# Key decay on ScalarE, weight conversion on GpSimd in eight rounds, and hidden slices moved inside the attention loop

## The chip, the cores and the metric

One Trainium2 chip, one of its cores. The metric is device time in microseconds for one execution of the whole kernel, the median of several executions. TensorE (PE) does matmuls, VectorE (DVE) and ScalarE (ACT) work on SBUF and PSUM, GpSimd (POOL) on SBUF, and SyncE (SP) issues the DMAs. Each engine runs its own list of instructions in order and waits for the others by semaphores. Float32 data goes through the matmuls as two rounded parts, a high part and a rest, each in TensorE's `float32r` type.

## The reference

```
q, k, v: (2 batches, 8 heads, 768 tokens, 64); lam: one decay per head
attention, in blocks of tokens:
    out  = (q k^T * lam^(i-j), lower triangle) v  +  (q * lam^(i+1)) state
    state = lam^block * state + (k * lam^(block-1-j))^T v
x (1536 x 512) = out, heads side by side
x  = G(x @ w_in (512 x 2048)) @ w_out          G: 0, (h+1)^2/4, h, piecewise
out = (sigmoid(x @ w_gate) * (x @ w_val)) @ w_out2      d_ff 1536
```

The five weight matrices come as float64 words and are turned into float32 parts on the chip.

## The kernel before

**Attention.** The work is cut into 16 units: two batches, four pairs of heads, two halves of the 768 tokens, each half three blocks of 128 tokens. For unit i: `pre_k` multiplies the keys by the decay column of the table `DT` (tile kd), `pre_q` the queries by `qp` (tile qs); `scores` makes q k^T on PE; `updates` makes the three state updates from kd; `weigh_states` multiplies the scores by `DT` into pT (two DVE instructions, one for each head) and runs the recurrence sc of the states on DVE, then copies them to st on ACT; `outputs` makes the unit's output x on PE from pT, qs and st; `evacuate` splits x into xh (ACT, line 492) and xl (DVE, line 493), the input of the feed-forward. The tables come from a small constant `cs`: `DT` and `qp` of the first two heads are built on chip, the others go through DRAM (`pd`) and come back by DMA.

**The order** is written out by hand: step i of the loop issues scores, updates and states of unit i+1, the decayed keys of unit i+2, then outputs and evacuation of unit i, then the decayed queries of unit i+2. Each engine keeps that order.

**Weight conversion.** The weights are 68 pieces of 128 x 512 words. `w_round` is a pipeline of one piece per stage: round k makes the words of piece k (two ACT copies), the float of piece k-1 (DVE lines 95 and 96, then an integer add, line 98, on DVE or POOL), and the two parts of piece k-2: the high part on ACT (line 102) and the rest (line 106, `w_low`) on DVE or POOL. In the attention loop `ROUNDS` says at which steps a round is issued; afterwards rounds go between the feed-forward's units.

**Feed-forward.** `feed_forward` is a generator of slices: a slice is one 128-wide strip of the hidden layer for 512 tokens, 12 matmuls (`hidden`, lines 150 to 152: high part, rest, high part with xl, for four strips of the input), then an activation (lines 176 to 178), a split of it (gh, gl: lines 168, 169), and `project`, 12 matmuls (line 205). `HIDDEN` says at which steps of the attention loop one slice is made ahead of time; there are four. The 24 matmuls of the first two projects come right after attention, and from there on PE runs the feed-forward.

Of the kernel before, what the change touches and what calls it, by code (L numbers as in the profile page):

```python
# [10 lines left out]
AF = mybir.ActivationFunctionType  # L11
ALU = mybir.AluOpType
PSUM = bass.MemoryType.PSUM

B, H, S, D = 2, 8, 768, 64
NT, DM = B * S, H * D
FF1, FF2 = 2048, 1536
P = 128
NP = H // 2
CU = 3  # L20
# [5 lines left out]
GF = 4  # L26
PADW = 64
CST = 4 + PADW + P
HIDDEN = (7, 9, 11, 13)
ROUNDS = (3, 4, 5, 6, 8, 9, 10, 11, 12, 13, 14)  # L30
NQD = 2
NEARLY = 4
WARM = 2
# [4 lines left out]
def fused_kernel(ctx: ExitStack, tc: tile.TileContext, qkv, qd, cst, w1, w2, out):  # L38
    nc = tc.nc
    pe, act, dve, pool, sp = nc.tensor, nc.scalar, nc.vector, nc.gpsimd, nc.sync  # L40
# [20 lines left out]

    pieces = [(n, o) for n in range(NF1 + NF2) for o in range(0, 1024 if n < NF1 else 1536, 512)]
    pieces[:8] = sorted(pieces[:8], key=lambda no: 2 * no[0] + (3 if no[1] else 0))
    index = {no: i for i, no in enumerate(pieces)}
    raws, ws, tmps = {}, {}, {}

# [3 lines left out]
    def w_load():  # L73
        i = prog["loaded"]
        if i >= len(pieces) or i >= NRAW + max(0, prog["round"] - 2):
            return
        prog["loaded"] += 1
        n, o = pieces[i]
        raws[i] = rawp.tile([P, 512], I64, tag="raw", name=f"raw{i}")
        src = w1[n] if n < NF1 else w2[n - NF1]  # L80
        sp.dma_start(out=raws[i], in_=src[:, o:o + 512])
# [190 lines left out]
    steps = feed_forward(rounds)  # L272


    with ExitStack() as actx:
# [6 lines left out]
        nu = len(units)  # L282
        raw_u = {}

        def u_load(i):
            if i >= nu:
                return
            b, p, h = units[i]
            if i < NEARLY:

                t = [wp.tile([P, 2, 512], F32, tag="w", name=f"u{i}_{j}")
                     .rearrange("p a b -> p (a b)")[:, 0:2 * UT]
                     .rearrange("p (a t) -> p a t", a=2) for j in range(2)]
                for j in range(2):
                    sp.dma_start(out=t[j], in_=qkv[b, p, h][:, 2 * j:2 * j + 2])
            else:
                a = up.tile([P, 4, UT], F32, tag="u", name=f"u{i}")
                sp.dma_start(out=a, in_=qkv[b, p, h])
                t = [a[:, 0:2], a[:, 2:4]]
            raw_u[i] = [t[j // 2][:, j % 2] for j in range(4)]  # L300
# [4 lines left out]
        DT = kp.tile([P, H, P], F32, name="DT")  # L305
# [15 lines left out]
        def tables():  # L321

            cs = tp.tile([P, 512], F32, tag="r", bufs=3, name="cs")
            dm = [tp.tile([P, 512], F32, tag="r", bufs=3, name=f"dm{j}")[:, 0:2 * (PADW + P)]
                  .rearrange("p (h x) -> p h x", h=2) for j in range(2)]
            act.dma_start(out=cs[:, 0:CST], in_=cst)
            for i in range(3):
                u_load(i)
            dve.memset(zero, 0.0)
            for j in range(2):  # L330
                dve.memset(dm[j][:, :, 0:PADW], 0.0)
            dve.memset(half, 0.5)
            pool.memset(pw[:, 0:P - 1], 0.0)
            pool.memset(pw[:, P - 1:P], 1.0)
            pool.memset(st[0], 0.0)
            act.activation(st[1], st[0], AF.Copy)

            act.activation(pw[:, P:P + 1], cs[0:H, 2:3], AF.Copy)
            for k in range(7):
                w = 1 << k  # L340
                act.activation(pw[:, P + w:P + 2 * w], pw[:, P:P + w], AF.Copy,
                               scale=pw[:, P + w - 1:P + w])
            act.dma_start(out=pd, in_=pw)
            act.activation(qp[:, 0, 0:1], cs[:, 3:4], AF.Copy)
            for k in range(7):
                w = 1 << k
                act.activation(qp[:, 0, w:2 * w], qp[:, 0, 0:w], AF.Copy,
                               scale=qp[:, 0, w - 1:w])
            sq = [cs[:, 0:2]] + [cs[:, CST + 2 * k:CST + 2 * k + 2] for k in range(6)]
            for k in range(1, 7):  # L350
                pool.tensor_tensor(out=sq[k], in0=sq[k - 1], in1=sq[k - 1], op=ALU.mult)
            for h in range(2):
                for k in range(7):
                    w = 1 << k
                    src = cs[:, 4:CST] if k == 0 else dm[k % 2][:, h]
                    dve.scalar_tensor_tensor(
                        out=DT[:, h] if k == 6 else dm[(k + 1) % 2][:, h, PADW:],
                        in0=src[:, PADW - w:PADW + P - w], scalar=sq[k][:, h:h + 1],
                        in1=src[:, PADW:], op0=ALU.mult, op1=ALU.add,
                    )  # L360
            pdv = pd[:, :]
            for e in range(2):
                sp.dma_start(
                    out=qp[e * D:(e + 1) * D, 1:],
                    in_=bass.AP(pdv.tensor, pdv.offset + (2 + e) * 2 * P + P,
                                [[0, D], [4 * P, NP - 1], [1, P]]),
                )
            for h0, h1 in ((2, 4), (4, H)):
                sp.dma_start(
                    out=DT[:, h0:h1],  # L370
                    in_=bass.AP(pdv.tensor, pdv.offset + h0 * 2 * P,
                                [[1, P], [2 * P, h1 - h0], [1, P]]),
                )
            u_load(3)
            u_load(4)
            w_load()
            u_load(5)
            w_load()

        S_ps, U_ps, pT, qs, kd, xs = {}, {}, {}, {}, {}, {}  # L380

        def pre_k(i):

            b, p, h = units[i]
            kd[i] = sp2.tile([P, CU, 2, D], F32, tag="kd", name=f"kd{i}")
            pool.tensor_tensor(
                out=kd[i], in0=raw_u[i][2].rearrange("p (c h d) -> p c h d", c=CU, h=2),
                in1=DT[:, 2 * p:2 * p + 2, P - 1:P].unsqueeze(1).to_broadcast([P, CU, 2, D]),
                op=ALU.mult,
            )  # L390

        def pre_q(i):

# [38 lines left out]
        def weigh_states(i):  # L432
            b, p, h = units[i]
            pT[i] = sp2.tile([P, 2, UT], F32, tag="pT", name=f"pT{i}")
            S, t = S_ps.pop(i), U_ps.pop(i)
            sb, sd = sc[p % 2], st[p % 2]
            n0, n1 = h * CU, min(h * CU + CU, 2 * CU - 1)

            def weigh(e):
                dve.tensor_tensor(  # L440
                    out=pT[i][:, e].rearrange("p (c t) -> p c t", c=CU),
                    in0=S[e][:, 0:UT].rearrange("p (c t) -> p c t", c=CU),
                    in1=DT[:, 2 * p + e].unsqueeze(1).to_broadcast([P, CU, P]), op=ALU.mult,
                )

            def state(n):
                u = t[:, (n - n0) * D:(n - n0 + 1) * D]
                if n == 0:
                    dve.tensor_copy(out=sb[:, n], in_=u)
                elif n < n1:  # L450
                    dve.scalar_tensor_tensor(  # L451
                        out=sb[:, n], in0=sb[:, n - 1], scalar=qp[:, p, P - 1:P], in1=u,
                        op0=ALU.mult, op1=ALU.add,
                    )

            weigh(0)
            state(n0)
            weigh(1)
            state(n0 + 1)
            state(n0 + 2)  # L460
            for e in range(2):
                r = slice(e * D, (e + 1) * D)
                act.activation(sd[r, n0:n1, r], sb[r, n0:n1], AF.Copy)  # L463
# [33 lines left out]

        with tc.manual_schedule():
            tables()
            warm()  # L500
            scores(0)
            scores(1)
            pre_k(0)
            pre_k(1)
            updates(0)
            weigh_states(0)
            pre_q(0)
            pre_q(1)


            for i in range(nu):
                if i + 1 < nu:
                    if i:
                        scores(i + 1)
                    updates(i + 1)
                    weigh_states(i + 1)
                if i + 2 < nu:
                    pre_k(i + 2)

                def finish():  # L520
                    outputs(i)
                    evacuate(i)

                if i in ROUNDS:
                    w_round(pool, finish, pool if i >= nu // 2 else dve)
                else:
                    finish()
                if i + 2 < nu:
                    pre_q(i + 2)
                u_load(i + 6)  # L530
                w_load()
                if i in HIDDEN:
                    next(steps)


    late = ctx.enter_context(tc.tile_pool(name="late", bufs=1, reuse_waits="tile"))
# [67 lines left out]
```

## Time and profile before

| | |
|---|---|
| median of 3 runs | 630.03 us (629.92 to 630.14) |
| profiled execution | 630.28 us, of which the span from first to last instruction is 628.3 |
| PE busy | 608.9 us, 97% of the span |
| DVE busy | 356.5 us, 57% |
| ACT busy | 287.8 us, 46% |
| POOL busy | 57.0 us, 9%, all in the first six of the page's 40 slices (94 us) |
| granted PE clock, mean | 0.991 of full speed |

A line of the trace gives the start, the duration, the engine, the source line, the operation and the tiles as out<-in. In brackets stands how long the engine sat idle before it and what ended that. Matmuls are pipelined: the duration of one is longer than the time to the next.

### The profile page before, as it was taken

To read this page: it belongs to the slowest core of one execution; us is meant where nothing else is said; L and a number is where in the kernel's file an instruction comes from. 1 tells how busy PE (TensorE), PEld (TensorE's weight loads), DVE (VectorE), ACT (ScalarE), POOL (GpSimd) and SP (SyncE) were. 2 spreads that over 40 slices of the span, in tenths; PEclk is the share of its full clock that TensorE was granted. 3 is DMA by queue.
4 is the path that set the end of the run, shared out by engine and by line. 5 is a ranking of instruction groups with operands and counts; after the bars stand their busy time and mean duration, and the time that the engine had idled before them with its cause. 6 is when DMAs were issued, how large, how long until landed. Compare 5 with 4: busy or idle time off the path is not lost.

```text
span 628.3 us, 7878 instructions
## 1 busy us (share of the span) xinstructions
PE 608.9 (97%) x3076; PEld 500.8 (80%) x3076; DVE 356.5 (57%) x613; ACT 287.8 (46%) x511; POOL 57.0 (9%) x62
## 2 busy tenths in 40 slices
PE   6978799999999999999999999999999999999997
PEld 4866588888888888888888888888888888888886
DVE  5678876465656665667577721256842167813132
ACT  5457766566546554656484511245631145311110
POOL 4568920000000000000000000000000000000000
PEclk8989999999999999999999999999999999999999
DMA  6967531021203111222222400024420022001011
GB/s 211 413 226 259 211 120 61 23 100 68 68 33 101 66 57 45 70 65 68 67 68 67 135 1 0 1 75 127 134 68 0 1 67 68 1 0 68 0 68 67
DMA packets 15813, 52.59 MB, mean 84 GB/s; under 512 B 1688, under 2 KB 2976, under 8 KB 15776
## 3 DMA queue, kind: packets, MB, share of 16 engines
q1 hardware_dynamic: 15616, 51.98, 24.9%
q8 instruction: 24, 0.39, 0.2%
q10 hardware_dynamic: 160, 0.11, 0.1%
q14 instruction: 13, 0.11, 0.0%
HBM read 48.92 MB, written 3.15 MB: 83 GB/s over the span
## 4 chain that ended last, share of the span: by engine, by line
PE 88%; DVE 6%; ACT 3%; issue 2%; DMA 1%; POOL 0%; ACTq 0%; POOLq 0%
PE a L205 36%; PE h L150 17%; PE h L152 17%; PE h L151 17%; DVE pT L440 2%; DVE sc L451 1%; ACT st L463 1%; ACT xh L492 1%; DMA cs<-in_cst 1%; DVE wr L96 0%; PE x L473 0%; DVE w L106 0%; DVE part L219 0%; DVE xl L493 0%; ACT w L102 0%
## 5 line engine op out<-in xcount | busy, mean ns | idle before, releaser
L150 PE MATMUL h<-xh,w 128*128 128x512 f32 x480 | 187.2, 390 | 1.7 <-ACT xh L492 1.7
L152 PE MATMUL h<-xl,w 128*128 128x512 f32 x480 | 186.9, 389 | 0.0
L151 PE MATMUL h<-xh,w 128*128 128x512 f32 x480 | 186.7, 389 | 0.0
L205 PE MATMUL a<-gh,w 128*128 128x512 f32 x384 | 118.5, 390 | 0.0
L150 PEld LDWEIGHTS h<-xh,w 128*128 128x128 f32 x480 | 90.1, 188 | 20.7 <-ACT xh L492 2.1
L152 PEld LDWEIGHTS h<-xl,w 128*128 128x128 f32 x480 | 90.1, 188 | 19.0 <-DVE xl L493 0.3
L151 PEld LDWEIGHTS h<-xh,w 128*128 128x128 f32 x480 | 90.1, 188 | 18.5
L184 DVE TENSOR_TENSOR r<-r,h 128x512 f32<-128x512 f32 x36 | 24.8, 688 | 138.8 <-PE h L152 138.8
L205 PE MATMUL a<-w,gh 128*128 128x512 f32 x288 | 88.6, 389 | 0.0
L205 PEld LDWEIGHTS a<-gh,w 128*128 128x128 f32 x384 | 71.9, 188 | 15.1 <-issue 0.2
L168 ACT ACTIVATE gh<-r 128x512 fp32r<-128x512 f32 x84 | 52.5, 625 | 63.3 <-DVE r L184 55.7
L178 DVE SCALAR_TENSOR_TENSOR r<-r,h 128x512 f32<-128x512 f32 x48 | 33.0, 687 | 84.6 <-ACT r L177 84.5
L205 PE MATMUL a<-gl,w 128*128 128x512 f32 x192 | 74.7, 389 | 0.0
L176 ACT ACTIVATE r<-h,half 128x512 f32<-128x512 f32 x48 | 33.0, 688 | 90.3 <-PE h L152 90.3
L169 DVE TENSOR_TENSOR gl<-r,gh 128x512 fp32r<-128x512 f32 x84 | 59.1, 704 | 16.6 <-ACT gh L168 16.6
L205 PEld LDWEIGHTS a<-w,gh 128*128 128x128 f32 x288 | 54.0, 188 | 11.2
L183 ACT ACTIVATE r<-h 128x512 f32<-128x512 f32 x36 | 21.5, 597 | 87.0 <-PE h L152 87.0
L102 ACT ACTIVATE w<-wr 128x512 fp32r<-128x512 f32 x68 | 42.3, 623 | 39.7 <-DVE wr L98 39.5
L205 PE MATMUL a<-w,gl 128*128 128x512 f32 x144 | 56.0, 389 | 0.0
L96 DVE SCALAR_TENSOR_TENSOR wr<-raw,wr 128x512 uint32<-128x512 uint32 x68 | 51.2, 753 | 2.3
L88 ACT ACTIVATE wr<-raw 128x512 f32<-128x512 f32 x68 | 45.1, 663 | 0.2 <-POOL w L106 0.2
L89 ACT ACTIVATE wc<-raw 128x512 int32<-128x512 uint32 x68 | 44.9, 660 | 0.0
(52 smaller groups left out, 507.2 us busy)
## 6 DMA issues: line engine op xcount, KB each, us to landing
raw<-in_w SPq DMA_DIRECT2D x68, 512.0 KB, 3.6
u<-in_qkv SPq DMA_DIRECT2D x12, 768.0 KB, 4.7
u<-in_qkv SPq DMA_DIRECT2D x8, 384.0 KB, 5.1
out<-part SPq DMA_DIRECT2D x12, 256.0 KB, 2.1
DT<-pd SPq DMA_DIRECT2D x1, 256.0 KB, 4.2
qp<-pd SPq DMA_DIRECT2D x2, 96.0 KB, 2.8
DT<-pd SPq DMA_DIRECT2D x1, 128.0 KB, 3.8
cs<-in_cst ACTq DMA_DIRECT2D x1, 98.0 KB, 4.1
```

The costliest lines, as they stand in the source:

```text
L88: act.activation(r, hi.bitcast(F32), AF.Copy, scale=2.0 ** -112)
L89: act.activation(c, lo, AF.Copy, scale=2.0 ** -29)
L96: dve.scalar_tensor_tensor(out=ru, in0=hi, scalar=0x80000000, in1=ru, op0=ALU.bitwise_and, op1=ALU.bitwise_or)
L102: act.activation(ws[i][:, 0], tmps[i][1], AF.Copy)
L150: pe.matmul(h, lhsT=wh, rhs=xh[:, k, tt], start=(k == 0), stop=False)
L151: pe.matmul(h, lhsT=wl, rhs=xh[:, k, tt], start=False, stop=False)
L152: pe.matmul(h, lhsT=wh, rhs=xl[:, k, tt], start=False, stop=(k == NP - 1))
L168: act.activation(gh, g, AF.Copy)
L169: dve.tensor_tensor(out=gl, in0=g, in1=gh.bitcast(F32), op=ALU.subtract)
L176: act.activation(r, h, AF.Relu, bias=half, scale=0.5)
L178: dve.scalar_tensor_tensor(out=r, in0=r, scalar=1.0, in1=h, op0=ALU.min, op1=ALU.max)
L205: pe.matmul(accs[j], lhsT=a, rhs=b_, start=(f == 0 and m == 0), stop=(f == GF - 1 and m == 2))
```

## The change

The constant `cs` is loaded first on SP's queue instead of on ACT's, and the fourth unit's inputs come before the tables' DMAs. The decayed keys of units 2 to 15 are two ACT instructions (one for each head) instead of one on POOL; those of units 0 and 1 stay on POOL, in two instructions. Eight rounds instead of eleven are issued in attention, all with integer add and rest on POOL, and the first eight pieces are ordered so that the four pieces for the hidden layer come first and those for the projects after. A slice is issued inside step i, between updates and states of unit i+1 and the outputs of unit i, at steps 8, 10, 12 and 14, and no longer at the end of steps 7, 9, 11 and 13. For the first unit, both weighings come before the states.

```diff
-HIDDEN = (7, 9, 11, 13)
-ROUNDS = (3, 4, 5, 6, 8, 9, 10, 11, 12, 13, 14)
+HIDDEN = (8, 10, 12, 14)
+ROUNDS = (3, 5, 7, 9, 11, 13, 14, 15)
...
-    pieces[:8] = sorted(pieces[:8], key=lambda no: 2 * no[0] + (3 if no[1] else 0))
+    pieces[:2 * GF] = sorted(pieces[:2 * GF], key=lambda no: (no[1], no[0]))
...
-            act.dma_start(out=cs[:, 0:CST], in_=cst)
-            for i in range(3):
+            sp.dma_start(out=cs[:, 0:CST], in_=cst)
+            for i in range(4):
                 u_load(i)
...
-            u_load(3)
             u_load(4)
-            w_load()
             u_load(5)
             w_load()
...
-            pool.tensor_tensor(
-                out=kd[i], in0=raw_u[i][2].rearrange("p (c h d) -> p c h d", c=CU, h=2),
-                in1=DT[:, 2 * p:2 * p + 2, P - 1:P].unsqueeze(1).to_broadcast([P, CU, 2, D]),
-                op=ALU.mult,
-            )
+            for e in range(2):
+                if i < 2:
+                    pool.tensor_tensor(
+                        out=kd[i][:, :, e],
+                        in0=raw_u[i][2].rearrange("p (c h d) -> p c h d", c=CU, h=2)[:, :, e],
+                        in1=DT[:, 2 * p + e, P - 1:P].unsqueeze(1).to_broadcast([P, CU, D]),
+                        op=ALU.mult,
+                    )
+                    continue
+                act.activation(
+                    kd[i][:, :, e],
+                    raw_u[i][2].rearrange("p (c h d) -> p c h d", c=CU, h=2)[:, :, e],
+                    AF.Copy, scale=DT[:, 2 * p + e, P - 1:P],
+                )
...
             weigh(0)
-            state(n0)
-            weigh(1)
+            if i:
+                state(n0)
+                weigh(1)
+            else:
+                weigh(1)
+                state(n0)
...
                     updates(i + 1)
-                    weigh_states(i + 1)
                 if i + 2 < nu:
                     pre_k(i + 2)
+                if i + 1 < nu:
+                    weigh_states(i + 1)
+                if i in HIDDEN:
+                    next(steps)
...
                 if i in ROUNDS:
-                    w_round(pool, finish, pool if i >= nu // 2 else dve)
+                    w_round(pool, finish, pool)
...
                 u_load(i + 6)
                 w_load()
-                if i in HIDDEN:
-                    next(steps)
```

POOL before, in the second third of the attention loop (wr and wc are a weight piece under conversion, w a finished piece; qs and kd are the decayed queries and keys):

```order
L98 TENSOR_TENSOR wr2_465<-wr2_465,wc2_466 128x512
L396 TENSOR_TENSOR qs8_519<-u8_330,qp_92 128x384
L386 TENSOR_TENSOR kd9_548<-u9_377,DT_91 128x384
L396 TENSOR_TENSOR qs9_562<-u9_377,qp_92 128x384
L386 TENSOR_TENSOR kd10_603<-u10_421,DT_91 128x384
L98 TENSOR_TENSOR wr3_514<-wr3_514,wc3_515 128x512
```

POOL of the change, at steps 9 to 13:

```order
L97 TENSOR_TENSOR wr2_553<-wr2_553,wc2_554 128x512
L105 TENSOR_TENSOR w1_660<-wr1_464,w1_660 128x512
L403 TENSOR_TENSOR qs11_667<-u11_470,qp_92 128x384
L403 TENSOR_TENSOR qs12_728<-u12_508,qp_92 128x384
L97 TENSOR_TENSOR wr3_662<-wr3_662,wc3_663 128x512
L105 TENSOR_TENSOR w2_771<-wr2_553,w2_771 128x512
```

The keys are gone from POOL, and a round puts two instructions there, the add of one piece and behind it the rest of the piece before.

PE before, around the first slice (x is a unit's output, h a slice, s the scores, uu the updates):

```order
L425 MATMUL uu_533<-u_330,kd_496 64x64 x6
L473 MATMUL x_550<-pT_489,u_291 64x128 x6
L482 MATMUL x_550<-qs_470,st_99 128x128 x3
L150 MATMUL h_0_0_566<-xh,w_463 128x512
L151 MATMUL h_0_0_566<-xh,w_463 128x512
L152 MATMUL h_0_0_566<-xl,w_463 128x512
```

PE of the change, around the first slice:

```order
L432 MATMUL uu_572<-u_381,kd_525 64x64 x4
L149 MATMUL h_0_0_587<-xh,w_551 128x512
L150 MATMUL h_0_0_587<-xh,w_551 128x512
L151 MATMUL h_0_0_587<-xl,w_551 128x512
...
L151 MATMUL h_0_0_587<-xl,w_551 128x512
L484 MATMUL x_604<-pT_528,u_333 64x128 x6
L493 MATMUL x_604<-qs_506,st_98 128x128 x2
```

The slice now stands ahead of a unit's outputs; before it stood behind them. Its second matmul (line 150 of the change) reads the rest of the weight piece.

DVE before, at the end of attention (pT and sc belong to the last unit, xl to the last two, wr_914 and wr_980 are pieces under conversion):

```order
L440 TENSOR_TENSOR pT_957<-s_1_945,DT 128x384
L451 SCALAR_TENSOR_TENSOR sc_97<-sc_97,qp,uu_952 128x64
L95 TENSOR_SCALAR wr_914<-wr_914 128x512
L96 SCALAR_TENSOR_TENSOR wr_914<-raw_751,wr_914 128x512
L493 TENSOR_TENSOR xl<-x_967,xh 128x384
L95 TENSOR_SCALAR wr_980<-wr_980 128x512
```

DVE of the change at the same place (gl and r are of slices, wr_882 and wr_948 are pieces):

```order
L458 SCALAR_TENSOR_TENSOR sc_97<-sc_97,qp,uu_899 128x64
L168 TENSOR_TENSOR gl_0_925<-r_0_822,gh_0_924 128x512
L177 SCALAR_TENSOR_TENSOR r_0_928<-r_0_928,h_0_0_911 128x512
L94 TENSOR_SCALAR wr_882<-wr_882 128x512
L95 SCALAR_TENSOR_TENSOR wr_882<-raw_562,wr_882 128x512
L504 TENSOR_TENSOR xl<-x_935,xh 128x384
L94 TENSOR_SCALAR wr_948<-wr_948 128x512
L95 SCALAR_TENSOR_TENSOR wr_948<-raw_671,wr_948 128x512
L504 TENSOR_TENSOR xl<-x_958,xh 128x384
```

The float steps of two pieces now stand behind the activation r of the last slice. The end of POOL's list in the change:

```order
L403 TENSOR_TENSOR qs_887<-u_669,qp 128x384
L97 TENSOR_TENSOR wr_882<-wr_882,wc_883 128x512
L105 TENSOR_TENSOR w_946<-wr_773,w_946 128x512
L97 TENSOR_TENSOR wr_948<-wr_948,wc_949 128x512
L105 TENSOR_TENSOR w_970<-wr_882,w_970 128x512
```

Here `w_946` and `w_970` are the pieces that the first two projects read; before, those projects read pieces of the rounds at steps 8 and 10.

## Rows read from the trace of the kernel before

**Rows 1.** Chain of waits, in order of time: start us, us, what.

```profile
0.74 4.11 DMA cs<-in_cst
...
19.69 0.50 ACT xh L492
...
26.28 0.50 ACT xh L492
...
42.65 0.50 ACT xh L492
...
72.89 0.49 ACT xh L492
...
81.17 4.81 PE a L205 x21
```

**Rows 2.** Busy time in two stretches: us, then each engine's, PEclk, DMA.

```profile
0.00:80.53 80.53, 64.87 (x675) 50.62 (x676) 61.27 (x134) 48.35 (x105) 54.56 (x61) 0.94 0.70 257
80.53:622.00 541.47, 541.47 (x2393) 448.42 (x2392) 292.54 (x476) 239.43 (x407) 2.45 (x2) 1.00 0.18 57
```

**Rows 3.** DMA issues of the page, by line, KB, us to landing.

```profile
out<-part SPq DMA_DIRECT2D x12, 256.0 KB, 2.1
```

**Rows 4.** Timeline of the start: start us, us, engine, line, what.

```profile
15.19 0.84 POOL L386 TENSOR_TENSOR kd<-u,DT 128x384 f32<-128x384 f32 x1 [0.98 <-DMA DT<-pd]
```

**Rows 5.** Groups of instructions on ACT by shape: busy us, mean ns.

```profile
L463 ACT ACTIVATE st<-sc 64x192 f32<-64x192 f32 x16 | 5.8, 362 | 12.7 <-DVE sc L451 12.5
...
L341 ACT ACTIVATE pw<-pw 8x64 f32<-8x64 f32 x1 | 0.3, 348 | 0.0
```

**Rows 6.** Timeline of 59 to 69 us, steps 10 to 12.

```profile
59.72 1.29 POOL L98 TENSOR_TENSOR wr<-wr,wc 128x512 int32<-128x512 int32 x1 [1.18 <-DVE wr L96]
...
60.75 0.40 PE L151 MATMUL h<-xh,w 128*128 128x512 f32 x1
...
60.96 1.29 POOL L106 TENSOR_TENSOR w<-wr,w 128x512 fp32r<-128x512 f32 x1
...
61.49 1.04 DVE L95 TENSOR_SCALAR wr<-wr 128x512 uint32<-128x512 uint32 x1
...
62.37 0.49 ACT L492 ACTIVATE xh<-x 128x384 fp32r<-128x384 f32 x1
...
62.89 0.63 ACT L102 ACTIVATE w<-wr 128x512 fp32r<-128x512 f32 x1
...
63.02 0.39 PE L152 MATMUL h<-xl,w 128*128 128x512 f32 x1
...
64.56 0.62 ACT L168 ACTIVATE gh<-r 128x512 fp32r<-128x512 f32 x1
...
68.48 0.63 ACT L463 ACTIVATE st<-sc 64x128 f32<-64x128 f32 x2 [2.07 <-DVE sc L451]
```

**Rows 7.** Timeline of 28 to 46 us, steps 3 to 8.

```profile
28.59 0.42 DVE L95 TENSOR_SCALAR wr<-wr 128x512 uint32<-128x512 uint32 x1
...
29.04 0.69 DVE L96 SCALAR_TENSOR_TENSOR wr<-raw,wr 128x512 uint32<-128x512 uint32 x1
...
29.88 1.28 POOL L98 TENSOR_TENSOR wr<-wr,wc 128x512 int32<-128x512 int32 x1 [1.43 <-PE x L473]
...
44.33 0.69 ACT L176 ACTIVATE r<-h,half 128x512 f32<-128x512 f32 x1 [1.19 <-PE h L152]
...
45.05 0.63 ACT L177 ACTIVATE r<-r 128x512 f32<-128x512 f32 x1
...
45.71 0.69 DVE L178 SCALAR_TENSOR_TENSOR r<-r,h 128x512 f32<-128x512 f32 x1 [1.98 <-ACT r L177]
```

**Rows 8.** Busy time in three short stretches, columns as in rows 2.

```profile
31.70:33.10 1.40, 0.00 (x0) 0.00 (x0) 1.33 (x4) 0.87 (x3) 1.40 (x2) 1.00 1.04 417
33.70:37.00 3.30, 3.30 (x26) 2.75 (x24) 3.30 (x7) 1.53 (x4) 3.19 (x3) 0.50 0.72 253
...
67.40:69.50 2.10, 0.00 (x0) 0.00 (x0) 2.07 (x6) 0.99 (x3) 2.10 (x3) 1.00 0.87 357
```

## The prediction

> **What bounds the kernel now.** First the chain of waits [rows 1]: up to about 80 us it changes engine at every piece (DVE, ACT, PE); from the row at 81.17 on it is PE alone. Then the table of stretches [rows 2]: from 80.53 to 622.00 PE is busy for 541.47 of 541.47 us, so nothing that ACT, DVE or POOL save there counts. The row at 81.17 holds 21 of the first two projects' 24 matmuls, at 4.81 / 21 = 0.229 us each; three had been slipped in earlier, so PE's continuous stretch starts in effect at 81.17 - 3 x 0.229 = 80.5. What the change is worth is how that point moves: as many slices (four) lie ahead of it, and as many matmuls behind it. Later stalls I count at nothing: three pieces fewer are ready at the start, but a round costs DVE under 3 us and DVE is busy 293 of 541 us there [rows 2].
>
> I follow X(i), the start of ACT's copy of unit i's output (line 492). In rows 1 X(1) is 19.69, X(3) 26.28, X(7) 42.65 and X(13) 72.89. That gives four stretches: start, 22.96 us from X(1) to X(7), 30.24 to X(13), 7.6 to the start of the continuous stretch.
>
> **The start.** The constant lands 4.11 us after its issue [rows 1]; the quickest landing in the profile is 2.1 [rows 3], so it can come up to 2.0 us earlier. But ACT now makes the decayed keys of unit 2, and they stand in its list ahead of the states of unit 1 and of X(0). They need a table that comes by DMA: POOL had to wait for it until 15.19 [rows 4], and a 768 KB load now goes before it on SP's queue. I take 0.5 us gained, between 0 (the table lands as before) and 2.0. The keys cost ACT two instructions of about 0.45: 0.36 for 192 columns without a scale read from SBUF, 0.35 for 64 with one [rows 5].
>
> **X(1) to X(7).** Units without a round took 26.28 - 19.69 = 6.6 us a pair [rows 1], three pairs 19.8. Rounds at 3, 5 and 7 fit inside: the floats run on DVE while ACT copies states and output, and words and keys run on ACT while DVE evacuates and weighs. Before, rounds at 3 to 6 stretched this to 22.96, among other things because DVE's line 95 takes 0.42 alone [rows 7] but 1.04 beside a POOL instruction (61.49, POOL's rest lasting until 62.25, [rows 6]). So 3.2 gained; if ACT's words and keys stick out by 0.3 at two steps, 2.6.
>
> **X(7) to X(13), the slices.** Here I see the price. Slice 0 needs piece 0, whose rest is made on POOL in the round of step 7, the step just before; likewise pieces 1, 2, 3 at steps 9, 11, 13. PE takes the slice ahead of the unit's outputs, so a slice that waits holds up everything behind it. Counted from X of the round's step: line 95 starts 0.88 earlier (61.49 against 62.37, [rows 6]); from its start to POOL's add it is 29.88 - 28.59 = 1.29 [rows 7]; add to rest 1.24 (59.72 to 60.96) and the rest 1.29 [rows 6]. So the rest is done at -0.88 + 1.29 + 1.24 + 1.29 = 2.9, and the slice's second matmul can start at 3.0. From the second to the last matmul's end it is 63.02 + 0.39 - 60.75 = 2.66 [rows 6]: 5.7. Then ACT's two activations, 45.71 - 44.33 = 1.38 with the step to DVE [rows 7], and the output's copy behind them in ACT's list: the next X comes 7.1 after the last. Without a slice a step takes 3.5 as above. A pair: 10.6; three pairs 31.8 against 30.24, 1.6 lost. Before, slices used weights that had been ready for steps, and the pairs cost as much because DVE and POOL were loaded with two rounds; the round saved is paid back in waiting. Bounds: none lost, if the copy is not held up by its full length, to 2.6 with the keys on ACT beside it.
>
> **X(13) to the continuous stretch.** The last slice ends at 5.7 after X(13), DVE's activation of it runs from 7.1 to 7.7. Only then come line 95 and 96 of the next piece (0.45 + 0.69, [rows 7]), POOL's add (8.95 to 10.2) and the rest of the first project's piece, until 11.5: its second matmul starts at 11.6. PE, done with the outputs at about 8.8, waits 2.7. The rest of the second project's piece follows after another add, at 14.0 at best; with DVE's floats held up by POOL as in rows 6, 14.7. The first project ends at 14.1, so up to 0.7 is added.
>
> DVE's held-up floats are where a page bears on the sum. In the Trainium skill, "SBUF — State Buffer", section "SBUF: two separate sides" says that DVE and POOL share a pair of ports as an exclusive lock that one holds for a whole instruction; 61.49 in rows 6 agrees, and that rule gives the 14.7, its absence the 14.0.
>
> I take 14.7; less 13 matmuls before it (2.95) the stretch starts in effect at X(13) + 11.8, against 7.6: 4.2 lost, between 3.4 and 4.4.
>
> **PE's clock.** PE stood still from 31.7 to 33.1 and the clock fell to half (0.50, 1.2 GHz) from 33.7 to 37.0; it also stood still from 67.4 to 69.5 and the clock stayed at 2.4 GHz [rows 8]. The change adds waits of about 3 us (first slice) and 2.7 us (first project), and three of some 1.7. A fall costs up to half of those 3.3 us, some 1.7. One fall in two for the two long waits: 1.7, between none and five (8.5).
>
> **Sum.** -0.5 - 3.2 + 1.6 + 4.2 + 1.7 = +3.8. The profiled execution took 630.28 (span 628.3, 2.0 around it): 634.1. The median of the runs is 0.25 lower than that execution: 633.8.
>
> **Rivals.** *The slices' wait is hidden* (faster). POOL has lost 14 key instructions; if its rest comes 1.5 us or more sooner than I count, ACT's list decides: from X(9) the copy and the high part with the words 2.2 (62.37 to 64.56), keys 0.8, states 0.65, the split 0.6, activations 1.4 [rows 6, 7], 5.6 for the step, 9.1 for the pair. Three pairs are 27.4, 4.4 less than counted; the projects' pieces follow 1.5 to 2 sooner: 633.8 - 1.7 - 4.4 - 2.1 = 625.6. For it: before, ACT stood idle 2.07 us waiting for states (68.48, [rows 6]), so there is air in this loop. Against it: the order puts the rest behind the add of the same round, and that add behind DVE.
>
> *The clock falls at every wait* (slower still): 633.8 + 4 x 1.7 = 640.6. The fall in rows 8 after the shorter of the two waits speaks for it, the other stretch against. The Trainium skill, "TensorE: Matmul & The Clock Gate", section "HAM oscillation — how this bites in real kernels", tells of a kernel whose clock fell at every wait between bursts of matmuls; in rows 8 only one wait of the two did this.
>
> *Gains and losses cancel* (no difference): the start gains its full 2.0 and no clock falls: 633.8 - 1.5 - 1.7 = 630.6. For it: tables and both weighings of unit 0 hang on the constant. Against it: the DMA'd table in ACT's list.
>
> **How the numbers follow.** My forecast has 0.57, with a range of its own of 631.5 to 637; the slices hidden 0.15, the clock at every wait 0.12, cancelling 0.16. A measurement of this kernel tells apart about 0.2%, 1.26 us, so "same" is 628.8 to 631.3. Faster: 0.16, the first rival and a little of the third. Same: 0.16, most of the third and the forecast's edge. Slower: 0.68. The range runs from 629.0, just outside the third rival, to 638.5, part of the way to the second; most of the first and half of the second, 0.2 together, lie outside.
>
> **What would show it.** Right: PE waiting about 2 us for POOL's rest (line 105 of the change) at the second matmul of each slice and some 2.7 at the first project; pairs of X near 10.6 from X(7) on; X(7) before 40 us; the continuous stretch starting 2 to 6 us later than 80.5. Wrong: slices that start without waiting for POOL, or pairs near 9; a first X at 14 us or less; or PE waiting for weights behind the first four projects, which I count at nothing.

## The result and the profile after

| | before | after |
|---|---|---|
| median | 629.97 us (629.63 to 630.14, 4 runs) | 637.92 us (636.21 to 638.47, 4 runs) |
| ratio | | 1.0122, 95% interval 1.0101 to 1.0144 |
| profiled execution, span | 630.28 us, 628.3 | 638.47 us, 636.7 |
| granted PE clock, mean | 0.991 | 0.987 |

The change makes the kernel slower by 7.95 us. The forecast was 3.8 us: the sign was right, the loss is twice as large. The prediction's four stretches can be measured in both traces. For the end of the last stretch I take the start of the first slice after the first two projects (85.81 before, 94.14 after), less the 5.44 us that 24 matmuls take at full clock (before, from 85.81 to 91.25, 12 of a slice and 12 of a project); that gives 80.37 and 88.70. The boundaries that are not shown elsewhere (timeline): X(1), X(13) and that slice in after, and the slice before.

```profile
20.70 0.49 ACT L503 ACTIVATE xh<-x 128x384 fp32r<-128x384 f32 x1
...
75.48 0.49 ACT L503 ACTIVATE xh<-x 128x384 fp32r<-128x384 f32 x1
...
94.14 0.39 PE L149 MATMUL h<-xh,w 128*128 128x512 f32 x1
```

```profile
85.81 0.39 PE L150 MATMUL h<-xh,w 128*128 128x512 f32 x1
```

| stretch | before | after | difference | forecast |
|---|---|---|---|---|
| start to X(1) | 19.69 | 20.70 | +1.0 | -0.5 |
| X(1) to X(7) | 22.96 | 20.02 | -2.9 | -3.2 |
| X(7) to X(13) | 30.24 | 34.76 | +4.5 | +1.6 |
| X(13) to the continuous stretch | 7.48 | 13.22 | +5.7 | +4.2 |
| PE's clock, in the two rows above | | | | +1.7 |
| sum | | | +8.3 (span: +8.4) | +3.8 |

Busy time in stretches of after (us, then busy time of PE, PEld, DVE, ACT and POOL, then the granted PE clock, DMA share and GB/s), to hold against [rows 2, 8]:

```profile
0.00:88.72 88.72, 69.63 (x680) 53.35 (x681) 51.70 (x128) 55.19 (x127) 34.84 (x45) 0.91 0.60 216
88.72:630.00 541.28, 541.28 (x2386) 448.36 (x2385) 298.97 (x486) 242.25 (x412) 1.92 (x2) 1.00 0.19 60
42.80:49.50 6.70, 5.80 (x19) 4.28 (x21) 0.31 (x2) 2.08 (x6) 1.81 (x2) 0.50 0.00 0
84.50:87.10 2.60, 0.09 (x1) 0.00 (x0) 2.57 (x3) 1.36 (x3) 2.55 (x2) 1.00 0.59 200
87.20:90.40 3.20, 3.12 (x7) 2.48 (x8) 3.17 (x4) 1.89 (x3) 2.48 (x3) 0.50 0.45 156
```

The second row is the feed-forward behind the first projects. PE is busy for all of it, as in [rows 2], so the whole difference arises ahead of it. In the first row DVE and POOL have less to do than before (51.70 against 61.27, 34.84 against 54.56) and ACT has more (55.19 against 48.35); no engine is busy for all of it, and the stretch is longer all the same. The last three rows show the clock: half speed (1.2 GHz) during the first slice, still 2.4 GHz while PE waits at 84.5 to 87.1, half speed again behind that wait.

Waits of PE after 38 us (engine and line, what ended the wait: total us, times, longest):

```profile
PE h L150 <- POOL w L105: 5.1, 4, 1.3
PE h L149 <- ACT w L101: 3.5, 4, 1.9
PE a L204 <- POOL w L105: 2.7, 1, 2.7
```

Each of the four slices waits for its weight piece twice: first for the high part from ACT, then, one matmul later, 1.3 us for the rest from POOL. The first project waits 2.7. No other wait of PE is listed there.

The chain of waits of after (start us, us, what) from the second matmul of the third slice to that of the fourth, and then to the first project; [rows 1] shows the chain of before:

```profile
67.76 0.50 PE h L150
...
70.58 0.69 ACT r L175
...
71.97 0.69 DVE r L177
72.65 0.47 DVE xl L504
73.12 0.46 DVE pT L447
...
75.06 0.70 DVE wr L95
...
75.89 0.81 POOL wr L97
...
77.13 1.28 POOL w L105
...
78.45 0.50 PE h L150
...
85.82 1.42 POOL w L105
...
87.28 7.03 PE a L204 x23
```

This is a ring. A slice ends on PE, ACT and DVE activate it, DVE then does its share of the next unit (xl, pT, the recurrence), only then the floats of the next piece; POOL adds and makes the rest; the next slice starts. Once round takes 78.45 - 67.76 = 10.69 us, two steps of the loop, and no engine is busy for all of it (PE, the busiest, for 8.88). The last row shows the slow clock too, which lasts for a part of it: 23 matmuls took 7.03 us, 0.306 each on average against 0.229 in [rows 1].

Timeline of after around the first slice (start us, us, engine, line, operation, tiles, in brackets the idle time before and what ended it):

```profile
40.72 0.49 ACT L503 ACTIVATE xh<-x 128x384 fp32r<-128x384 f32 x1
...
41.92 0.49 PE L149 MATMUL h<-xh,w 128*128 128x512 f32 x1 [1.87 <-ACT w L101]
...
42.38 1.27 POOL L105 TENSOR_TENSOR w<-wr,w 128x512 fp32r<-128x512 f32 x1
...
43.70 0.79 PE L150 MATMUL h<-xh,w 128*128 128x512 f32 x1 [1.29 <-POOL w L105]
...
48.80 0.69 ACT L175 ACTIVATE r<-h,half 128x512 f32<-128x512 f32 x1 [4.60 <-PE h L151]
...
50.64 0.49 ACT L503 ACTIVATE xh<-x 128x384 fp32r<-128x384 f32 x1 [0.50 <-PE x L493]
```

From X(7) at 40.72 the rest is done at 43.65 (forecast 2.9 after X, measured 2.93) and the second matmul starts at 2.98 (forecast 3.0). From that matmul to the activation it then takes 48.80 - 43.70 = 5.1 us, against 70.58 - 67.76 = 2.8 in the third slice at full clock. X(8) comes 9.92 after X(7), not 7.1.

At the start, SP's and ACT's DMA issues and ACT's first work in after (timeline):

```profile
0.74 0.39 SPq L325 DMA_DIRECT2D cs<-in_cst  x1
...
5.36 0.54 ACTq L342 DMA_DIRECT2D pd<-pw  x1
...
10.89 1.32 SPq L362 DMA_DIRECT2D qp<-pd  x2
...
15.93 0.80 ACT L393 ACTIVATE kd<-u,DT 128x192 f32<-128x192 f32 x2 [4.42 <-DMA DT<-pd]
...
17.27 0.49 ACT L503 ACTIVATE xh<-x 128x384 fp32r<-128x384 f32 x1
```

and the same issues before:

```profile
7.49 0.53 ACTq L343 DMA_DIRECT2D pd<-pw  x1
...
9.77 1.32 SPq L363 DMA_DIRECT2D qp<-pd  x2
```

The constant now lands in 2.0 us (4.11 in [rows 1]) and the powers `pd` go out 2.1 us earlier. But SP issues the tables only when `pd` has been written, and that is 5.53 us later (5.36 to 10.89) where it was 2.28. The table is there at about 15.9 for ACT; in [rows 4] POOL had it at 15.19. What was gained at the front was lost on the way through DRAM.

### The profile page after: what moved, and what is told of

Same layout as the page of the kernel before. It is cut to its first block, busy times and chain, and to the rows that moved or that the text cites. A ratio compares the mean times of both kernels' runs of the same rounds, so it can differ in the third digit from the quotient of the medians.

```text
span 636.7 us, 7908 instructions
## 1 busy us (share of the span) xinstructions
PE 613.8 (96%) x3076; PEld 503.8 (79%) x3076; DVE 353.4 (56%) x617; ACT 297.4 (47%) x539; POOL 36.8 (6%) x46
## 4 chain that ended last, share of the span: by engine, by line
PE 86%; DVE 1%; POOL 1%; ACT 0%; issue 0%; POOLq 0%
PE a L204 36%; PE h L150 17%; PE h L151 17%; PE h L149 17%; DVE part L218 0%; POOL w L105 0%; POOL wr L97 0%; DVE wr L95 0%; ACT r L175 0%; ACT r L176 0%; DVE pT L447 0%; DVE wr L94 0%; DVE r L177 0%; DVE xl L504 0%; DVE sc L458 0%
## 5 line engine op out<-in xcount | busy, mean ns | idle before, releaser
L204 PE MATMUL a<-gh,w 128*128 128x512 f32 x384 | 119.9, 393 | 2.7 <-POOL w L105 2.7
L168 DVE TENSOR_TENSOR gl<-r,gh 128x512 fp32r<-128x512 f32 x84 | 57.7, 687 | 16.8 <-ACT gh L167 16.8
L95 DVE SCALAR_TENSOR_TENSOR wr<-raw,wr 128x512 uint32<-128x512 uint32 x68 | 49.0, 721 | 2.3
```

What stands on the lines that cost most here:

```text
L95: dve.scalar_tensor_tensor(out=ru, in0=hi, scalar=0x80000000, in1=ru, op0=ALU.bitwise_and, op1=ALU.bitwise_or)
L168: dve.tensor_tensor(out=gl, in0=g, in1=gh.bitcast(F32), op=ALU.subtract)
L204: pe.matmul(accs[j], lhsT=a, rhs=b_, start=(f == 0 and m == 0), stop=(f == GF - 1 and m == 2))
```

## The experiments

The theory after the result: (1) with the rounds of the change each slice needs a piece that is finished in the step just before, so the loop runs in the ring above, at 10.7 us a pair; (2) the long waits of PE bring its clock down, which costs some 3 us more; (3) the start loses 1 us because of the loads ahead of the tables. The rivals: the slice's place inside the step is itself dear; the keys on ACT make the steps long; the clock is a small matter. For "before" in the runs below the medians are 630.39, 630.62 and 630.45 us.

**Rounds one to two steps earlier.** The five rounds in the middle, among them the four that finish the slices' pieces, move by two steps: the rest of the first slice's piece is made at step 5 instead of step 7, for a slice at step 8. The first round and the last two move by one.

```diff
-ROUNDS = (3, 5, 7, 9, 11, 13, 14, 15)
+ROUNDS = (2, 3, 5, 7, 9, 11, 13, 14)
```

> The changed kernel with its eight rounds one to two steps earlier: at 2, 3, 5, 7, 9, 11, 13, 14 instead of 3, 5, 7, 9, 11, 13, 14, 15, nothing else. Theory (the slices and the first projects wait for weight rests that POOL finishes just in time, and the clock falls while PE waits): no wait for POOL's rest at the slices, X(7) to X(13) falls from 34.8 to 27 to 29 us, the way from X(13) to the continuous stretch from 13.4 to about 9, the clock does not fall at the slices; 626 to 628 us in all. Rival (the slice's place ahead of the outputs, and the keys in ACT's list, make the pairs long): pairs stay near 10.6, only the projects' wait goes; 632 to 635 us.

Measured: 623.51 us (623.38 to 624.38), ratio to before 0.9889 (0.9872 to 0.9905). This one line turns the loss of 8 us into a gain of 7, more than I expected (626 to 628 us). X(7) to X(13) takes 26.41 us (34.76 in after), X(13) to the continuous stretch 12.2 less 24 matmuls, 6.8 (13.2). The chain of waits of this kernel:

```profile
49.84 0.49 ACT xh L503
...
51.00 0.57 ACT wr L87
...
52.13 0.69 ACT kd L393 x2
...
53.36 0.64 ACT gh L167
54.02 1.42 DVE gl L168
55.44 0.60 DVE r L177
...
58.87 0.49 ACT xh L503
```

The ring is gone: neither POOL nor PE stands in the chain any more, a pair is 9.0 us (49.84 to 58.87), and ACT's and DVE's lists set it in turn. PE waits once after 38 us:

```profile
PE a L204 <- POOL w L105: 1.7, 1, 1.7
```

With the same place of the slices and the same keys on ACT, theory 1 stands and both rivals on place and keys fall. The granted clock is full from 22.5 us to the end of the work here, so part of the 14.4 us between the two kernels is clock, which the next runs separate.

**PE kept busy in the waits.** Idle matmuls are put ahead of the waiting ones: 9 before the first slice, 4 before each of the next three, 10 before the first project. What they write is overwritten by the matmuls behind them.

```diff
+    def filler(b, count):
+        for _ in range(count):
+            pe.matmul(b, lhsT=xh[:, 0, 0:P], rhs=xh[:, 0, 0:TT], start=True, stop=True)
...
+        filler(h, {0: 9, 1: 4, 2: 4, 3: 4}.get(n, 0) if (t, o) == (0, 0) and n < GF else 0)
...
+            if u == (0, 0, 0, 0) and j == 0:
+                filler(accs[0], 10)
```

> The changed kernel with idle matmuls in PE's list where it waits: nine ahead of the first slice, four ahead of each other slice, ten ahead of the first project, written to the bank that the next matmul clears. The waits for the weight rests stay. Theory (the falls of the clock after the long waits cost 2.8 us at the first slice and 1.6 at the first project): the clock stays at 2.4 GHz there, X(7) to X(8) falls from 9.9 to 7.2, in all 633 to 634.5 us. Rival (the waits alone make the loss, the clock only slows matmuls that something else holds up): 637 to 638.5 us.

Measured: 634.70 us (634.50 to 634.94), ratio to before 1.0067 (1.0052 to 1.0082): just above the 633 to 634.5 us that I expected, and 3.2 us less than after, though PE got more work, and runs that lie within 0.4 us of each other where those of after spread over 2.3. Its first slice (timeline):

```profile
39.76 2.33 PE L144 MATMUL h<-xh 128*128 128x512 f32 x9
41.93 0.39 PE L154 MATMUL h<-xh,w 128*128 128x512 f32 x1
43.50 0.50 PE L155 MATMUL h<-xh,w 128*128 128x512 f32 x1 [1.18 <-POOL w L105]
```

and the stretch in which after had half speed, in this kernel (columns as above):

```profile
42.72:49.55 6.83, 6.05 (x63) 4.88 (x63) 2.02 (x6) 3.74 (x10) 2.70 (x3) 1.00 0.19 59
```

The wait for POOL is still there (1.18), the fall is not: the granted clock is 1.00 there, and full from 20.0 us to the end of the work. X(7) to X(8) takes 7.27 (forecast 7.1), X(7) to X(13) 32.20, X(13) to the continuous stretch 12.51. Against after the clock thus cost 34.76 - 32.20 = 2.56 us in the slices and 13.22 - 12.51 = 0.7 at the projects, 3.3 together. Theory 2 holds. What remains is the loss without these falls: 4.3 us, which is what the forecast's other terms should have given and gave as 2.1.

**The fourth unit's inputs behind the tables again.**

```diff
-            for i in range(4):
+            for i in range(3):
                 u_load(i)
...
+            u_load(3)
             u_load(4)
```

> The changed kernel with the fourth unit's loads behind the tables' DMAs again, as before the change; the constant stays first on SP's queue. Theory (the small table passes through DRAM beside 0.77 MB more of unit loads, so it comes late, and ACT's keys of unit 2 wait for it ahead of the first output): the table lands near 14 instead of 15.8, X(0) falls from 17.3 to about 15.5, the rest is unchanged; 636 to 636.5 us. Rival (X(0) hangs on PE and the units, or a later unit 3 holds up the loop): no change or slower, 638 us or more.

Measured: 638.19 us (636.52 to 638.34), ratio 1.0116 (1.0101 to 1.0131), no difference from after. The tables are issued at 10.04 instead of 10.89 and X(1) comes at 20.42 instead of 20.70. My expectation was wrong: most of the delay of `pd` stays.

**The constant on ACT's queue and the units' inputs in the order of before.**

```diff
-            sp.dma_start(out=cs[:, 0:CST], in_=cst)
-            for i in range(4):
+            act.dma_start(out=cs[:, 0:CST], in_=cst)
+            for i in range(3):
...
-            u_load(4)
-            u_load(5)
+            for i in range(3, 6):
+                u_load(i)
```

> The changed kernel with the constant's load on ACT's queue and the unit loads in the order of before: three units, then the tables, then the fourth. Theory (with the constant 2 us earlier the tables' first transfer to DRAM only waits longer beside the unit loads, so the early constant buys nothing at the first outputs): X(1) within 0.5 of the changed kernel's 20.7, in all 637 to 639 us. Rival (the early constant does bring the units forward): X(1) later by 1 us or more, 639 to 640 us.

Measured: 637.54 us (636.80 to 637.80), ratio 1.0108 (1.0093 to 1.0123). `pd` goes out at 7.21 and the tables at 9.50, 2.29 later, as before; X(1) is 19.93. ACT's keys of unit 2 and 3 in this kernel (timeline):

```profile
15.15 0.80 ACT L393 ACTIVATE kd<-u,DT 128x192 f32<-128x192 f32 x2 [1.43 <-PE x L493]
...
17.93 0.80 ACT L393 ACTIVATE kd<-u,DT 128x192 f32<-128x192 f32 x2 [0.95 <-DMA u<-in_qkv]
```

ACT waits for the table at neither. So the early constant with its loads is worth nothing; X(1) without it is 0.8 us sooner, more than the 0.5 that I allowed, but kernels with one and the same start differ by as much (below). In the time it does not show: the granted clock fell once more than in after here (77.4 to 80.8 us), and X(13) to the continuous stretch took 14.6.

**Only two units' inputs ahead of the tables.**

```diff
-            for i in range(4):
+            for i in range(2):
...
-            u_load(4)
-            u_load(5)
+            for i in range(2, 6):
+                u_load(i)
```

> The changed kernel with only two units' loads ahead of the tables' transfers, the third and fourth behind them. Theory (unit loads hold up the transfer of the powers to DRAM, and with it the tables): the powers land 2 to 3 us earlier, SP issues the tables by 8.5 instead of 10.9, the table lands near 13.5 instead of 15.8, X(1) falls from 20.7 to 18.7 to 19.5; 636 to 637 us. Rival (the tables' small rows take their time whatever stands beside them, or unit 2 now comes too late): X(1) at 20.4 or later, no change.

Measured: 638.86 us (637.71 to 640.05), ratio 1.0131 (1.0112 to 1.0150): no gain, where I expected 636 to 637. The start of this kernel (timeline):

```profile
8.36 1.32 SPq L362 DMA_DIRECT2D qp<-pd  x2
...
10.89 2.14 SPq L294 DMA_DIRECT2D u<-in_qkv  x4
...
17.09 0.80 ACT L393 ACTIVATE kd<-u,DT 128x192 f32<-128x192 f32 x2 [5.53 <-DMA u<-in_qkv]
```

With less in front, `pd` is written 2.96 us after its issue (5.40 to 8.36) and the tables come 2.5 us sooner. That confirms the cause of their delay; but now the inputs of unit 2 are late, X(1) is 21.88. Here what brought the tables forward held the inputs back. Over all the kernels of this document the tables are issued at 8.2 to 8.4 us with two units' inputs ahead of them, at 9.5 to 10.0 with three, whether `pd` goes out at 5.4 or at 7.2 to 7.5, and at 10.1 to 11.1 with four: here the loads in front, not its own issue, set when the small write was done.

**Keys of units 2 to 15 on POOL again.**

```diff
+            if i >= 2:
+                pool.tensor_tensor(
+                    out=kd[i], in0=raw_u[i][2].rearrange("p (c h d) -> p c h d", c=CU, h=2),
+                    in1=DT[:, 2 * p:2 * p + 2, P - 1:P].unsqueeze(1).to_broadcast([P, CU, 2, D]),
+                    op=ALU.mult,
+                )
+                return
```

> The changed kernel with the decayed keys of units 2 to 15 on POOL again, in one instruction. Theory (on ACT the keys cost only at the start, where they wait for the table ahead of the first output; on POOL they run in its idle time ahead of a round): X(0) falls by 1 to 1.8 us, pairs stay within 0.4 of 10.7, and 636 to 637.5 us in all. Rival (two ACT instructions of 0.45 us in each of 14 steps lengthen every step): 10 us less, below 630. Second rival (on POOL they push the rests later): pairs 1 us longer, 640 or more.

Measured: 638.67 us (637.15 to 639.71), ratio 1.0128 (1.0112 to 1.0144): no gain, where I expected 636 to 637.5. X(0) falls from 17.27 to 12.76, so the keys in ACT's list did hold it back; but X(1) is 19.98, 0.7 sooner at most, because the keys wait for the table on POOL as well:

```profile
15.28 0.84 POOL L384 TENSOR_TENSOR kd<-u,DT 128x384 f32<-128x384 f32 x1 [3.26 <-DMA DT<-pd]
```

From X(1) to X(7) it takes 20.69 against 20.02, X(7) to X(13) 34.83 against 34.76. Where the ring sets the pace the keys' engine did not matter.

**Both: earlier rounds and keys on POOL.** The edits of the first and of the last kernel together.

> The changed kernel with rounds at 2, 3, 5, 7, 9, 11, 13, 14 and the keys of units 2 to 15 on POOL: what the keys' move is worth once no slice waits. Theory (POOL has room for them ahead of the rounds, ACT has room too): within 1.5 us of the 623.5 of the same rounds with the keys on ACT. Rival (POOL's key beside DVE's floats holds both up again, as before the change): 2 us or more slower, 625.5 to 628.

Measured: 623.22 us (622.45 to 625.62), ratio 0.9892 (0.9868 to 0.9916): the same as with the rounds alone. In the times the move of the keys is worth nothing in either kernel. The trace shows that here this is a balance and not the absence of an effect: with the keys on POOL X(1) comes at 18.78 instead of 20.97 and the pairs between X(9) and X(13) take 8.6 us instead of 9.0, but PE waits 2.38 us for a key of POOL at 36.69, with half speed behind it (38.4 to 41.7), and X(8) is only 0.25 us sooner.

**Earlier rounds and fewer loads first.** ROUNDS = (2, 3, 5, 7, 9, 11, 12, 13), and two units' inputs ahead of the tables as above.

> Meant to beat both: the changed kernel with two units' loads ahead of the tables and rounds at 2, 3, 5, 7, 9, 11, 12, 13. Theory: no slice and neither of the first two projects waits for a rest of POOL (1.7 us at the second project with the last rounds at 13 and 14), and the start gains 1 to 2 us: 620.5 to 622.5 us. Rival (the round at 12 stands beside a slice and lengthens that step by what the project wins): 623 us or more.

Measured: 624.96 us (624.74 to 625.33), ratio 0.9911 (0.9896 to 0.9926), 1.4 us more than the rounds alone and above the 620.5 to 622.5 that I expected. X(1) is 21.50 (20.97 there), and the pair from X(11) to X(13) takes 10.0 (8.95 there) with a round at step 12 in it; the late rounds' wait of 1.7 us at the second project is gone, which gives back 0.6. A new wait stands in its place: PE waits 1.4 us for the last unit's queries, which stand on POOL behind the rest of the round at step 13.

**Earlier rounds with the constant and the loads as before.** The edits of the first and the fourth kernel together.

> The rounds one step earlier as in the run before (623.51 us), and the constant on ACT's queue with three units' inputs ahead of the tables, as in the kernel before the change. Theory (the powers' way to DRAM and back waits among the loads, so the early constant buys nothing and the later position of the tables costs about 1 us): ACT's copy of unit 1's output starts at about 20.0 instead of 20.97, and all of it is kept up to the continuous stretch: 622.5 us, 622.0 to 623.0. Rival (the later steps absorb it: unit loads or the weight pieces decide from step 3 on): 623.5 as with the rounds alone. Second rival (the clock falls in the loop again, since the earlier steps shift against it): 625 or more.

Measured: 623.36 us (622.55 to 623.73), ratio 0.9886 (0.9872 to 0.9899). X(1) is 20.37, 0.6 sooner, and the continuous stretch starts 0.67 sooner in the profiled run, but the medians differ by 0.15 us, which is nothing: the 622.0 to 623.0 that I expected did not come. Theory 3 is not settled by the times. By X(1), which is 19.69 (before), 19.93 and 20.37 with the old loads and 20.70, 20.97, 20.94 and 20.11 with the new (after, the earlier rounds, the filled kernel and the next one, whose starts are the same), the mean is 20.0 against 20.7 with an overlap. One and the same start thus gave X(1) anywhere within 0.9 us, and the tables' issue between 10.06 and 11.10, so a part of the +1.0 in the table above may be the chance of one execution.

**Filled at the slices, not at the first project.** As the filled kernel, without the 10 matmuls.

> The changed kernel with idle matmuls ahead of the four slices (9, 4, 4, 4) but none before the first project. Theory (a clock fall at the slices costs some 2.5 us, the one at the first project only 0.7, because the second project's piece was late by 0.4 anyway): slices as in the filled run, 32.2 us from unit 7's copy to unit 13's, 13.2 from there to the continuous stretch: 635.4 us, 635.0 to 635.9, against 634.70 with both filled and 637.92 with none. Rival (a fall costs its full half at each place, 1.7 at the first project): 636.4. Second rival (only the first fall prepares the second, so none is left): 634.7 or a little less.

Measured: 635.25 us (634.05 to 635.54), ratio 1.0074 (1.0060 to 1.0087), as expected. The five runs fall in two groups: 634.05 and 634.09, mean clock 0.997, and 635.25 to 635.54, clock 0.992 to 0.995. The profile is of one of the first group; two stretches of it, PE's wait ahead of the first project and what follows:

```profile
80.90:83.60 2.70, 0.10 (x1) 0.00 (x0) 2.67 (x3) 1.39 (x3) 2.64 (x2) 1.00 0.52 193
83.70:86.60 2.90, 2.90 (x12) 2.15 (x12) 2.87 (x4) 1.83 (x3) 2.25 (x2) 1.00 0.48 165
```

The same wait (2.68 us here, 2.69 in after) left the clock at 2.4 GHz in this run and was followed by half speed in after. The difference between the groups, 1.2 to 1.5 us, is what this one fall may cost in a run; that it is the fall, and not the start, is read from the mean clock alone, and in the filled kernel runs of 0.993 and 0.997 took the same time (634.52 and 634.50), so it is not shown.

## Why the prediction was too low

**Its direction and its mechanism held.** The slice that waits for POOL's rest, the pair and the first project came out as worked out: the rest 2.93 us after X (2.9), the pair 10.7 (10.6) for the second and third pair, the first project's second matmul 87.28 - 75.48 = 11.80 after X(13) (11.6). X(1) to X(7) gained 2.9 (3.2). The range, 629.0 to 638.5, held the time. Not all of the prediction's own signs came: PE waits 1.3 us at the second matmul of a slice where about 2 was named, with 0.5 to 1.9 ahead of the first; X(7) is 40.72 and not before 40, and the continuous stretch starts 8.2 us later than 80.5 where 2 to 6 was named.

**The step that failed is the term on PE's clock:** "One fall in two for the two long waits: 1.7". Both long waits were followed by half speed, and the first fall lasted 6.8 us, twice the 3.3 on which I had based the price. By the filled kernel the falls cost 2.6 us at the slices and 0.7 at the projects, 3.3 in all: 1.6 more than forecast. [rows 8] holds one fall, and the price took its length for that of every fall; where half speed lasted 3.4 us, X(7) to X(8) was 1.5 us longer than without a fall (8.80 against 7.27), close to the 1.7, and where it lasted 6.8, 2.65 longer. The rival "the clock falls at every wait" was wrong in its mechanism: the three short waits, 1.3 us on POOL with 0.5 on ACT before it, never brought the clock down in after (in the kernel with the constant on ACT half speed from 77.4 to 80.8 us does lie in the fourth slice). The Trainium skill, "TensorE: Matmul & The Clock Gate", section "HAM oscillation — how this bites in real kernels", tells of a kernel whose clock fell at every wait for data between bursts of matmuls; the trace of after agrees at its two long waits (1.9 with 1.3 us behind it, and 2.7), and not at the three short ones.

**The start** was put at -0.5 between 0 and -2.0 and was +1.0, outside the bounds and 1.5 off, nearly as large an error, though up to 0.9 of it may be chance, as said above. I had named the danger ("a 768 KB load now goes before it") and then bounded it by "the table lands as before". The wrong thought was that the constant's gain and the table's landing are one chain with a fixed length: between them lies the 8 KB write of `pd`, which took 2.28 us among the loads before and 5.53 after. The run with two units first shows the loads as the cause (2.96); that the delay cost time in the end, no run shows.

**The remaining terms** were 1.5 us too low together: X(1) to X(7) by 0.3 (in after the clock was at half speed until 22.1 us; in the filled kernel, with full speed from 20.0, this stretch took 19.56 against 20.02, so this 0.3 can be clock too), the slices without falls by 0.4 (32.20 - 30.24 = 2.0 against 1.6), and the last stretch by 0.8 (12.51 - 7.48 = 5.0 against 4.2). The last is the second project's piece: its rest was ready 88.02 - 72.70 = 15.3 us after X(13) in the filled kernel where I had 14.7. DVE's float steps of the round that makes it, in that kernel (timeline); POOL's add of the same round, which stands ahead of the rest, waits for them:

```profile
82.05 1.34 DVE L94 TENSOR_SCALAR wr<-wr 128x512 uint32<-128x512 uint32 x1
83.42 1.65 DVE L95 SCALAR_TENSOR_TENSOR wr<-raw,wr 128x512 uint32<-128x512 uint32 x1
```

I had counted the first as held up by POOL, as in [rows 6], and the second at its 0.69 alone [rows 7]; beside POOL's rest (83.05 to 84.53) it took 1.65. The step without a slice, put at 3.5 "as above", would have been 3.3 by the 6.6 a pair above it; it took 3.44, so nothing hung on that. The five errors add up: 1.6 + 1.5 + 0.3 + 0.4 + 0.8 = 4.6, the span's 8.4 less the forecast's 3.8.

**The rival "the slices' wait is hidden"** gave 9.1 us a pair with ACT's list as the bound. It comes close to the kernel with earlier rounds, where a pair takes 9.0 (8.4 to 9.0 over the three) and the time is 623.5 (625.6 by the rival), but there the chain runs through DVE for nearly half of the pair. For the change as made it was wrong for the reason given: the rest stands behind the add of its own round, and that behind DVE. What I had not seen is that this closes a ring: DVE's floats wait behind the activation of the slice before, so PE's wait puts off the cause of the next one, and the move of the keys, which lie outside the ring, changed nothing there (34.83 against 34.76 us with the keys on POOL).

## What to carry to other kernels

When work made ahead of time is consumed, count how many steps lie between its last instruction and its reader: here two steps more, a single line, were worth 14 us of 638; whether one would have been enough, no run shows. Follow the chain until it returns to where it began; if it does, the ring's length is the period, and busy shares say nothing of it. An earlier load is a gain only if what stands behind it on the way, here an 8 KB write through DRAM, is not delayed by the loads that moved with it.

## What the hardware showed that I had not expected

- A wait of PE does not settle by its length whether the clock falls: 2.69 us before the first project was followed by half speed in after, 2.68 us at the same place by full speed in the kernel filled at the slices.
- The same wait before the first slice cost very different times by the clock alone: from X(7) to X(8) it takes 7.27 us with no fall, 8.8 where half speed lasted 3.4 us (the fourth unit later, the constant on ACT, and two units first) and 9.92 where it lasted 6.8 (after).
- A write of 8 KB to DRAM took from 2.28 us (before) to 5.79 us (earlier rounds) until it could be read back, depending on which loads were in flight.
- DVE's two float steps took 0.42 and 0.69 us alone [rows 7], and 1.34 and 1.65 beside POOL's add and rest in the filled kernel.
